# Q products of three chunks of layer 2 in a seven-product form, and other queue orders in which VectorE's and GpSimd's norms exclude each other

## The chip, the cores and the metric

The kernel runs on one core of one Trainium2 chip. The metric is device time in microseconds, the median of several executions. The core has five engines with their own instruction queues: TensorE (matmuls, PE in the profile; PEld are its weight loads), VectorE (DVE), ScalarE (ACT), GpSimd (POOL) and SyncE (SP), which issues the DMAs here. They meet only at semaphores.

## The reference

Four layers on 2048 tokens of 512 features: linear attention with 32 heads of 16, a feed-forward block with 1376 hidden features, and the same two again with the same weights. Each has a layernorm ahead of it and adds its result to x.

```python
qkv = (x @ wqkv).reshape(B, S, 3, H, Dh).transpose(2, 0, 3, 1, 4)
q, k, v = qkv[0], qkv[1], qkv[2]
phi = lambda t: where(t > 0, t + 1, exp(t)) + 1e-6
pq, pk = phi(q), phi(k)
kv = einsum("bhsd,bhse->bhde", pk, v)
z = einsum("bhsd->bhd", pk)
num = einsum("bhqd,bhde->bhqe", pq, kv)
den = einsum("bhqd,bhd->bhq", pq, z)[..., None] + 1e-6
attention = (num / den).transpose(0, 2, 1, 3).reshape(B, S, D) @ wo

x = x + attention(layernorm(x), wqkv, wo)
x = x + maximum(layernorm(x) @ w1, 0) @ w2
x = x + attention(layernorm(x), wqkv, wo)
return x + maximum(layernorm(x) @ w1, 0) @ w2
```

## The kernel before

Everything stays in SBUF. The 2048 tokens are 16 tiles of 128, in 4 chunks of 512. Layers are numbered 0 to 3: 0 and 2 are attention, 1 and 3 feed-forward. In names such as `2.q1_3` the first number is the layer; then come chunk and block. Tiles: `xn` holds normalized tokens (tokens on partitions), `Tb` the same transposed, `big` the results of the chunk at hand (phi(K), phi(Q), hidden units, and four spare units of a chunk, `rb_unit`), `ps` the eight PSUM banks, `escr` scratch, `Mf` the 512x512 matrix that the attention's end multiplies with.

**An attention layer.** Per chunk: K (`a_k`, four groups of four 512-column matmuls, `Tb` stationary), Q (`a_q`, four groups, `wqkv` stationary, all 512 tokens of the chunk as columns), and the sums G = xn^T phi(K) (`a_g`). phi takes three or four operations (`phi_evac`): ScalarE writes t + 1 (`_lin`) and exp(t) (`_exp`) from PSUM, VectorE cuts the exponential (`_em`) and takes the larger (`_phi`). When all K are done, G goes through wv (`a_kv`, into a bank from which VectorE's masked copy makes `KVT`, `kvmask`) and through wo (`a_m`) into `Mf`. The divisors are products with `Zc` (`a_den`), ScalarE's ln and exp of them (`lnd`, `rdc`), a DMA that spreads them over partitions (`spread`), and a multiplication of phi(Q) (`pqs`). Then `a_fin_chunk` multiplies with `Mf` and adds to x.

**A feed-forward layer.** The second product (`b_out_chunk`), and the first one of six of the eight chunks (`b_h_halves`), are done in a seven-product form: a product of 2 x 2 blocks with seven block products instead of eight, with sums of the operands' blocks made ahead on VectorE (`fs_`, `ts`, `ws_`, `sw`). One unit of it takes two banks Y and R and a chain: products 1 and 5 into Y, two copies by ScalarE (one of them seeds R), products 2 and 6, an addition on VectorE in PSUM, products 3 and 7, another addition, product 4. Two banks of results come out.

**The order.** The program records every operation with what it reads and writes, and `_list_schedule` makes the queue of each engine: on each, strictly by `prio`, which is an operation's place in the program plus its entry in the table `HINTS` (about 1700 entries). The table `ON` says on which of two engines a movable operation runs (evacuations with relu, norms, copies of G). Of VectorE's operations it marks some as `lock` and of GpSimd's some as `hog`: in the planner's clock a `lock` that would start during a `hog` begins at its end. Nothing at run time enforces that; there are only the queues and the semaphores.

The operations of two neighbouring layers are interleaved: layer 2's first chunks are on TensorE while layer 1's last are.

Of the kernel before, what the change touches and what calls it, by code (L numbers as in the profile page):

```python
# [7 lines left out]
ALU = alu_op_type.AluOpType  # L8
# [53 lines left out]
C_DVE_SC = 520.0  # L62
H_PLAIN = {(3, 0): 2}
# [7 lines left out]
HINTS = {"0.ainv": 7469, "0.ainvs": 7592, "0.apos": 6448, "0.apow": 6789, "0.apows": 7312, "0.as1": -3606, "0.as3": 3550, "0.as_h1":  # L71
# [377 lines left out]
def _list_schedule(ops, tile_ops, vbank, nbanks=8, full=(), seeded=()):  # L449
# [45 lines left out]
    while remaining:  # L495
# [78 lines left out]
        else:  # L574
            q = pool_op[0]
            held = 0.0
            if o.lock and q is not None and q.hog and q.t_start < st < q.t_done - TAIL[POOL]:
                held = q.t_done - TAIL[POOL] - st
# [1313 lines left out]
```

## Time and profile before

| | us |
|---|---|
| median of 3 runs (lowest, highest) | 267.24 (267.15, 267.86) |
| the profiled execution, its own time | 267.75 |
| its span, first to last instruction | 266.0 |
| TensorE busy, matmuls (1890) | 260.9 |
| VectorE busy (557 instructions) | 215.4 |
| ScalarE busy (420) | 192.0 |
| GpSimd busy (131) | 51.2 |

The granted TensorE clock was 1.000 over the span. The page cuts the span into 40 slices, a digit for the busy tenths of each (9 is 90% or more):

```profile
PE   7999999999999999999999999999999999999996
DVE  4897986799889999879786848479999888697865
ACT  4798899998975756898718689578599974656300
POOL 6410010012860023400001340001734040000000
```

A row of the groups reads: line, engine, operation, out<-in, shapes, count, busy us and mean ns of one, idle time of the engine ahead of them and what ended it. A row of the timeline reads: start, length, engine, line, operation, shapes, count, and in brackets the idle time ahead of it. A row of a window reads: the stretch, its length, and for PE, PEld, DVE, ACT and POOL the busy us with the count; then the clock and the DMA's share. Matmul rows include the pipeline's tail, so that neighbouring rows overlap.

### The profile page before, as it was taken

Reading aid. Unit: us, or ns where it says so; the run is one execution under the profiler, and the core shown is the slowest. Engines: PE = TensorE matmul, PEld = TensorE weight load, DVE = VectorE, ACT = ScalarE, POOL = GpSimd, SP = SyncE. Lnnn points to the kernel's source line nnn. Section 1 sums busy time; section 2 is a strip of 40 time slices with the busy share of each in tenths; the row PEclk is TensorE's granted clock in tenths of the full one; section 3 lists DMA queues with packets and bytes.
Section 4 is the critical chain, followed back from the end, with each engine's and each line's share of the span. In section 5 each row is a group of like instructions: output and inputs, shape, how many; then the busy total and the mean of one; then the engine's idle time right before and its main releaser. Section 6 shows DMA issues by size and latency. Waiting matters only on the chain.

```text
span 266.0 us, 5120 instructions
## 1 busy us (share of the span) xinstructions
PE 260.9 (98%) x1890; PEld 171.2 (64%) x1890; DVE 215.4 (81%) x557; ACT 192.0 (72%) x420; POOL 51.2 (19%) x131
## 2 busy tenths in 40 slices
PE   7999999999999999999999999999999999999996
PEld 3344444644755888767776744474488888888874
DVE  4897986799889999879786848479999888697865
ACT  4798899998975756898718689578599974656300
POOL 6410010012860023400001340001734040000000
PEclk9999999999999999999999999999999999999999
DMA  6744489866249023150000313054460501602104
GB/s 213 252 88 81 139 159 366 229 156 100 44 87 160 0 21 58 25 99 1 2 0 0 66 27 68 4 140 111 107 120 2 99 2 38 140 2 70 52 1 160
DMA packets 48122, 23.22 MB, mean 87 GB/s; under 512 B 38784, under 2 KB 45920, under 8 KB 48096
## 3 DMA queue, kind: packets, MB, share of 16 engines
q1 hardware_dynamic: 48096, 22.88, 37.2%
q8 instruction: 15, 0.25, 0.4%
q14 instruction: 11, 0.09, 0.1%
HBM read 7.14 MB, written 2.10 MB: 35 GB/s over the span
## 4 chain that ended last, share of the span: by engine, by line
PE 91%; DMA 4%; DVE 3%; SPq 1%; issue 0%; DVEq 0%
PE ps L928 91%; DMA xin<-in_A_x_dram 3%; DMA Tb<-xn 1%; DVE bst L802 1%; DVE big L921 1%; DVE xn L845 0%; DVE wqkv L944 0%; SPq L750 0%; SPq L744 0%; DVE escr L914 0%; DVE xn L1610 0%; DVE mv L803 0%; DVE veps L809 0%; DVEq L1822 0%
## 5 line engine op out<-in xcount | busy, mean ns | idle before, releaser
L928 PE MATMUL ps<-Tb,w 128*128 128x256 f16 (+2 forms) x240 | 42.0, 301 | 0.0
L1327 ACT ACTIVATE big<-ps 128x512 bf16<-128x512 f32 x58 | 33.0, 597 | 10.3 <-PE ps L928 10.0
L960 ACT ACTIVATE sqscr<-xres 128x512 bf16<-128x512 f32 x48 | 29.9, 626 | 9.6 <-DVE xres L954 9.4
L928 PE MATMUL ps<-w,big 128*128 128x256 bf16 (+5 forms) x213 | 36.5, 293 | 0.0
L928 PE MATMUL ps<-wqkv,Tb 128*128 128x512 bf16 x144 | 34.5, 379 | 0.9 <-DMA wqkv<-in_A_wqkv_dram 0.6
L928 PE MATMUL ps<-big,xn 128*128 128x512 bf16 (+1 forms) x160 | 31.2, 336 | 0.2 <-DVE veps L809 0.2
L910 ACT ACTIVATE big<-ps 128x512 bf16<-128x512 f32 x48 | 28.7, 603 | 1.5 <-PE ps L928 1.4
L928 PEld LDWEIGHTS ps<-Tb,w 128*128 128x128 f16 (+1 forms) x240 | 23.2, 98 | 9.3
L928 PE MATMUL ps<-xn,xin 128*128 128x256 f16 x168 | 28.8, 272 | 0.0
L1274 DVE TENSOR_TENSOR ps<-ps,escr 128x256 f32<-128x256 f32 x56 | 22.8, 427 | 7.1 <-PE ps L928 6.6
L912 ACT ACTIVATE escr<-ps 128x512 bf16<-128x512 f32 x44 | 25.7, 604 | 3.4 <-PE ps L928 3.3
L928 PE MATMUL ps<-Tb,wqkv 128*128 128x512 bf16 x112 | 27.1, 379 | 0.0
L825 POOL TENSOR_SCALAR mean<-s 128x4 f32<-128x4 f32 (+1 forms) x13 | 3.7, 285 | 117.4 <-DVE xres L954 117.3
L928 PE MATMUL ps<-Mf,big 128*128 128x512 bf16 x112 | 25.0, 379 | 0.0
L928 PEld LDWEIGHTS ps<-wqkv,Tb 128*128 128x128 bf16 x144 | 13.7, 98 | 16.5 <-DMA wqkv<-in_A_wqkv_dram 1.1
L928 PEld LDWEIGHTS ps<-w,big 128*128 128x128 bf16 (+1 forms) x213 | 20.3, 98 | 5.2
L928 PEld LDWEIGHTS ps<-big,xn 128*128 128x128 bf16 x160 | 15.1, 98 | 12.1 <-POOL xn L979 0.7
L928 PE MATMUL ps<-xin,big 128*128 128x256 bf16 x150 | 20.8, 272 | 0.0
L914 DVE TENSOR_SCALAR escr<-escr 128x512 bf16<-128x512 bf16 x52 | 14.3, 286 | 6.7 <-ACT escr L912 6.5
L928 PEld LDWEIGHTS ps<-Mf,big 128*128 128x128 bf16 x112 | 10.7, 98 | 12.7 <-DVE big L1105 0.3
L921 DVE TENSOR_TENSOR big<-big,escr 128x512 bf16<-128x512 bf16 x46 | 18.4, 417 | 0.2
L928 PEld LDWEIGHTS ps<-Tb,wqkv 128*128 128x128 bf16 x112 | 10.8, 98 | 11.7 <-issue 0.4
(139 smaller groups left out, 499.4 us busy)
## 6 DMA issues: line engine op xcount, KB each, us to landing
big<-rdc SPq DMA_DIRECT2D x32, 128.0 KB, 2.7
wqkv<-in_A_wqkv_dram SPq DMA_DIRECT2D x3, 512.0 KB, 5.0
w<-in_B_w_dram SPq DMA_DIRECT2D x1, 1376.0 KB, 7.6
w<-in_B_w_dram SPq DMA_DIRECT2D x1, 1280.0 KB, 10.8
xin<-in_A_x_dram SPq DMA_DIRECT2D x2, 512.0 KB, 4.5
out_dram<-wqkv SPq DMA_DIRECT2D x2, 512.0 KB, 3.5
xin<-in_A_x_dram SPq DMA_DIRECT2D x2, 256.0 KB, 6.2
wo<-in_A_wo_dram SPq DMA_DIRECT2D x1, 512.0 KB, 7.6
```

The costliest lines, as they stand in the source:

```text
L802: g.add(DVE, lambda e: e.bn_stats(bst[:, i, :], xin[:, i, :]), [("xin", i)] + list(after), [("bst", i)], C_DVE_BNST, name="bnst%d" % i)
L825: g.add(POOL, lambda e: e.tensor_scalar(mean[:, sl], s1[:, sl], -INV_D, None, ALU.mult), [("s1", i) for i in tl], [("mean", i) for i in tl ...
L910: g.add(ACT, lambda e: e.activation(dst_ap, psv[:, b, :], ACTF.Identity, bias=1.0 + 1e-6, scale=sc), [("ps", b)] + rk, [dst_key], C_ACT_PS ...
L912: g.add(ACT, lambda e: e.activation(esc, psv[:, b, :], ACTF.Exp, scale=sc), [("ps", b)] + rk, [ekey], C_ACT_EXP + xd, name=name + "_exp")
L914: g.add(DVE, lambda e: e.tensor_scalar(esc, esc, 1.0, 1e-6, ALU.min, ALU.add), [ekey], [ekey], C_DVE_BF4X, name=name + "_em")
L921: g.add(DVE, lambda e: e.tensor_tensor(dst_ap, dst_ap, esc, ALU.max), [dst_key, ekey], [dst_key], 340.0, name=name + "_phi")
L928: last = e.matmul(o, l, r, start=st, stop=sp, skip_group_check=skip)
L960: g.add(ACT, lambda e: e.activation(sqscr[:, q, :], xres[:, i, :], ACTF.Square, accum_out=s2[:, i:i + 1]), [("xres", i)], [("sqscr", q), ( ...
L1274: g.add(DVE, lambda e: e.tensor_tensor(psv[:, bank, 256:512], psv[:, Y, 0:256], m5, ALU.add), [("ps", Y), ("escr", s)], [("ps", bank)], C_ ...
L1327: g.add_flex([(ACT, lambda e: e.activation(unit_ap(u), psv[:, b, :], ACTF.Relu), C_ACT_PSUM), (DVE, lambda e: e.tensor_scalar(unit_ap(u), ...
```

## The change

1. In layer 2 the Q products of chunks 0, 1 and 2 (`QS`) take the seven-product form: `qk_chunk` in place of `a_q`. The blocks are: features in halves (0 to 255, 256 to 511), output columns in halves, and tokens of the chunk in halves. A chunk is two units (`qk_unit`, c = 0 and 1), each of which makes two of the four blocks of 128 output columns for all 512 tokens. The sums of the weights (`qk_weight_sums`, `swq1` to `swq4`, bf16, into `Mf`) are made once, during layer 1; the sums of the tokens (`qk_token_sums`, `ts0_1` and so on) for each of the three chunks, into the spare units of `big`. Chunk 3's Q, all K (`KS` is empty) and layer 0 stay as they were.
2. The planner marks every VectorE norm as `lock` (before, only those under 345 ns by its table, the norms of layer 0's start), only where the operation really runs on VectorE, and GpSimd's memset and selects of the start as `hog`. It takes 2100 instead of 1700 ns for the load of half of wq and wk, and 1000 instead of 800 for one load of x.
3. `HINTS` and `ON` are new throughout, so the order on every engine differs in all four layers.

```diff
--- before.py
+++ after.py
+KS = ()
+QS = (0, 1, 2)
...
-HINTS = {"0.ainv": 7469, "0.ainvs": 7592, "0.apos": 6448, "0.apow": 6789, "0.apows": 7312, "0.as1": -3606, "0.as3": 3550, "0.as_h1":
...
+HINTS = {"0.ainv": 7056, "0.ainvs": 9513, "0.apos": 6691, "0.apow": 7029, "0.apows": 7087, "0.as1": -9951, "0.as3": 4807, "0.as_h1":
...
-        self.lock = eng == DVE and dur < 345.0 and (name.endswith(("_em", "_phi")) or name[:4] in ("cent", "norm", "wvle")) or eng == DVE and (name[:3] in ("fs_", "ws_", "ts0", "ts1", "ts2", "ts3") or name[:2] == "sw" or name[:3] == "wsc")
-        self.hog = eng == POOL and name[:4] in ("norm", "fs_0", "fs_1", "fs_2", "fs_3")
+        self.lock = eng == DVE and dur < 345.0 and (name.endswith(("_em", "_phi")) or name[:4] in ("cent", "wvle")) or eng == DVE and (name[:4] == "norm" or name[:3] in ("fs_", "ws_", "ts0", "ts1", "ts2", "ts3") or name[:2] == "sw" or name[:3] == "wsc")
+        self.hog = eng == POOL and name[:4] in ("norm", "fs_0", "fs_1", "fs_2", "fs_3", "ms_h", "as_h")
...
-            if o.lock and q is not None and q.hog and q.t_start < st < q.t_done - TAIL[POOL]:
+            if e == DVE and o.lock and q is not None and q.hog and q.t_start < st < q.t_done - TAIL[POOL]:
...
-                [], [("wk", k), ("wq", k)], 1700.0, "ld_wqk%d" % k, late=(0.0, 300.0)[k])
-        ld_x(1, 0, 2, 800.0)
+                [], [("wk", k), ("wq", k)], 2100.0, "ld_wqk%d" % k, late=(0.0, 300.0)[k])
+        ld_x(1, 0, 2, 1000.0)
...
+        def qk_w(kind, k):
+            off, sums, key = (0, Mf, "Mf") if kind == "q" else (D, rdc, "rdc")
+            if k in (1, 2, 4):
+                d0, f0 = {1: (0, 0), 2: (2, 0), 4: (2, 256)}[k]
+                return wqkv[:, d0:d0 + 2, off + f0:off + f0 + 256], [("w" + kind, d0 // 2)]
+            q = {3: 4, 5: 1, 6: 2, 7: 3}[k]
+            return sums[:, q - 1, :].rearrange("p (d n) -> p d n", n=256), [(key, q - 1)]
...
+        def qk_weight_sums(kind):
+            off, key = (0, "Mf") if kind == "q" else (D, "rdc")
+            lf, ll, hf, hl = (wqkv[:, d:d + 2, off + f:off + f + 256] for d in (0, 2) for f in (0, 256))
+            lo, hi = [("w" + kind, 0)], [("w" + kind, 1)]
+            sm = {q: qk_w(kind, {4: 3, 1: 5, 2: 6, 3: 7}[q])[0] for q in range(1, 5)}
+            for q, a, b, op, rd in ((1, ll, hl, ALU.add, lo + hi), (3, lf, ll, ALU.subtract, lo),
+                                    (2, sm[1], lf, ALU.subtract, lo + [(key, 0)]), (4, hf, sm[2], ALU.subtract, hi + [(key, 1)])):
+                g.add(DVE, lambda e, q=q, a=a, b=b, op=op: e.tensor_tensor(sm[q], a, b, op), rd, [(key, q - 1)], C_DVE_TSUM, name="sw%s%d" % (kind, q))
+
+        def qk_block(t, r, c):
+            return Tb[:, 4 * t + 2 * c:4 * t + 2 * c + 2, 2 * r:2 * r + 2, :]
...
+        def qk_ts(t, q):
+            return unit_ap(rb_unit(t, q - 1)).rearrange("p (i d k) -> p i d k", i=2, d=2)
+
+        def qk_token_sums(t):
+            def flat(ap):
+                return ap.rearrange("p i d k -> p i (d k)")
+            lo, hi = qk_keys(t, 0), qk_keys(t, 1)
+            for q, a, b, rd in ((1, qk_block(t, 0, 1), qk_block(t, 0, 0), lo + hi), (2, qk_block(t, 1, 1), qk_ts(t, 1), hi + [("big", rb_unit(t, 0))]),
+                                (4, qk_block(t, 1, 0), qk_ts(t, 2), lo + [("big", rb_unit(t, 1))]), (3, qk_block(t, 1, 1), qk_block(t, 0, 1), hi)):
+                g.add(DVE, lambda e, q=q, a=a, b=b: e.tensor_tensor(flat(qk_ts(t, q)), flat(a), flat(b), ALU.subtract), rd, [("big", rb_unit(t, q - 1))],
+                      C_DVE_TSUM, name="ts%d_%d" % (t, q))
+
+        def qk_unit(t, kind, c):
+            Y, R = alloc_bank(True), alloc_bank(seeded=True)
+            s = scr_state["e"] % NSCR
+            scr_state["e"] = (s + 1) % NSCR
+            m5 = escr[:, s, :].bitcast(F32)
+            tag = "%s%d_%d" % (kind, t, c)
+
+            def prod(k, bank, half, start=False):
+                if k in (1, 2, 3):
+                    r_, c_ = {1: (0, 0), 2: (1, 0), 3: (1, 1)}[k]
+                    x, xk = qk_block(t, r_, c_), qk_keys(t, c_)
+                else:
+                    q = {4: 4, 5: 1, 6: 2, 7: 3}[k]
+                    x, xk = qk_ts(t, q), [("big", rb_unit(t, q - 1))]
+                w, wk = qk_w(kind, k)
+
+                def mk():
+                    o = psv[:, bank, 256 * half:256 * half + 256]
+                    if kind == "q":
+                        return [(o, w[:, d, 128 * c:128 * c + 128], x[:, :, d, :], start and d == 0, False, True) for d in range(2)]
...
+                mm_group(mk, xk + wk, [("ps", bank)], 2 * C_MM256, "%sp%d_%d_%d" % (kind, t, c, k))
...
+            def add(bank, n):
+                g.add(DVE, lambda e: e.tensor_tensor(psv[:, bank, 256:512], psv[:, Y, 0:256], m5, ALU.add),
+                      [("ps", Y), ("escr", s)], [("ps", bank)], C_DVE_HALF, name="%sa%d" % (tag, n))
+
+            def evac(bank, h):
+                if kind == "q":
+                    u = pq_unit(c + 2 * h, t)
+                    phi_evac(bank, unit_ap(u), ("big", u), "q%d_%d" % (t, c + 2 * h))
+                    return
...
+            def s0():
+                prod(1, Y, 0, True)
+                prod(5, Y, 1)
+                copy(lambda: psv[:, R, 0:256], 0, [("ps", Y)], [("ps", R)], tag + "c")
+                copy(lambda: m5, 1, [("ps", Y)], [("escr", s)], tag + "m")
+
+            def s1():
+                prod(2, R, 0)
+                prod(6, Y, 0)
+                add(R, 0)
+
+            def s2():
+                prod(3, R, 1)
+                prod(7, Y, 0)
+                evac(R, 0)
+                add(Y, 1)
+
+            def s3():
+                prod(4, Y, 0)
+                evac(Y, 1)
+            return s0, s1, s2, s3
+
+        def qk_chunk(t, kind):
+            a, b = qk_unit(t, kind, 0), qk_unit(t, kind, 1)
+            for f in (a[0], a[1], b[0], a[2], b[1], a[3], b[2], b[3]):
+                f()
...
                 def p1(t):
-                    for i in FIRST_ORDER if t == 0 and first_layer else range(4 * t, 4 * t + 4):
-                        a_k(i)
+                    if not first_layer and (t in KS or t in QS):
+                        qk_token_sums(t)
+                    if not first_layer and t in KS:
+                        qk_chunk(t, "k")
+                    else:
+                        for i in FIRST_ORDER if t == 0 and first_layer else range(4 * t, 4 * t + 4):
+                            a_k(i)
...
+                        return
+                    if not first_layer and t in QS:
+                        qk_chunk(t, "q")
                         return
                     a_q(t)
...
                 def o_step(t):
                     if layer == 1 and t == 0:
                         scale_weights()
+                    if layer == 1 and t == 0:
+                        for kind, used in (("k", KS), ("q", QS)):
+                            if used:
+                                qk_weight_sums(kind)
                     b_out_chunk(t, last_layer)
```

More of the change, by code (lines that the diff above doesn't have):

```diff
@@ L580, in _list_schedule @@
             o.t_done = st + o.dur + held + TAIL[e]
-            if o.lock:
+            if e == DVE and o.lock:
                 if st + held > train[1] + 10.0:
@@ L587, in _list_schedule @@
             q = pool_op[0]
-            if q is not None and (o.lock and not held or e == POOL):
+            if q is not None and (e == DVE and o.lock and not held or e == POOL):
                 fin = q.t_done - TAIL[POOL]
@@ L895, in transpose_pe, with phi_evac @@
             part(0, 4, ("T", i), str(i))
-        def phi_evac(b, dst_ap, dst_key, name, tok=None):
+        def phi_evac(b, dst_ap, dst_key, name, tok=None, shaped=lambda a: a):
+            dst_keys = dst_key if isinstance(dst_key, list) else [dst_key]
             n_scr = NSCR + NSCR0 if g.layer == 0 else NSCR
@@ L909, in phi_evac @@
             if not stt:
[L910 to L911 removed]
+                g.add(ACT, lambda e: e.activation(dst_ap, shaped(psv[:, b, :]), ACTF.Identity, bias=1.0 + 1e-6, scale=sc),
+                      [("ps", b)] + rk, dst_keys, C_ACT_PSUM + xd, name=name + "_lin")
             g.add(ACT, lambda e: e.activation(esc, psv[:, b, :], ACTF.Exp, scale=sc),
```

22 lines of the change are left out of this document (15 added, 7 removed), and 554 rows, old and new, of tables (HINTS, ON).

## The prediction

> **What bounds the kernel now.** I read the page's head first, then the chain of waits, then who waits for whom on TensorE, then the order of time where a term needs a price.
>
> ```profile
> span 266.0 us, 5120 instructions
> PE 260.9 (98%) x1890; PEld 171.2 (64%) x1890; DVE 215.4 (81%) x557; ACT 192.0 (72%) x420; POOL 51.2 (19%) x131
> ...
> 16.75 3.86 DMA Tb<-xn
> ...
> 20.65 242.27 PE ps L928 x1790
> ...
> PE ps L928 <- DMA Tb<-xn: 0.3, 1, 0.3
> ...
> PEld ps L928 <- DVE ps L1274: 0.5, 3, 0.2
> ```
>
> A busy share of 98% alone proves little, since the ends of matmuls are modelled. The chain says more: after the transpose that lands at 20.65 it consists of 1790 TensorE instructions in one piece, 242.27 us long. In the list of waits from 20.65 on, TensorE itself has one entry, 0.3 us, that same transpose. The weight loads do wait (0.5 us for the additions of the existing seven-product units, three times), but a weight load runs ahead of its matmul, and the matmul stream shows no gap. So the time is: start-up, plus the matmul columns, plus a tail. Fewer columns shorten it one for one; a wait of the matmul stream lengthens it one for one; VectorE and ScalarE cost nothing until TensorE waits for them.
>
> **The change, part by part: the columns.** The Q products of chunks 0 to 2 in layer 2 are 12 groups of four 512-column matmuls, 48 in all. In their place stand 6 units of 7 products of 2 matmuls of 256 columns, 84 in all.
>
> ```profile
> 22.39 3.62 PE L928 MATMUL ps<-Tb,wqkv 128*128 128x512 bf16 x16
> 25.84 1.03 PE L928 MATMUL ps<-big,xn 128*128 128x512 bf16 x4
> ...
> 174.35 1.47 PE L928 MATMUL ps<-big,xn 128*128 128x256 bf16 x12
> 175.66 0.28 PE L928 MATMUL ps<-GT,wqkv 128*128 128x128 bf16 x2
> ```
>
> Each row's length includes the pipeline's tail, so I go from start to start. Sixteen Q matmuls of layer 0 take 25.84 − 22.39 = 3.45 us, 0.2156 each; twelve of 256 columns take 1.31 us, 0.1092 each. Removed 48 × 0.2156 = 10.35, added 84 × 0.1092 = 9.17: **−1.18 us**. Half of 0.2156 per 256 columns would make it −1.29; that is its other end.
>
> The Trainium skill, "TensorE: Matmul & The Clock Gate", section "Back-to-back issue gap", speaks against this: it gives a sustained spacing of 131 ns at 512 columns and 81 ns at 128, and calls the 216 ns of a 512-column matmul an isolated figure. By a straight line between its two figures (98 ns at 256, an estimate) the exchange would be 84 × 98 − 48 × 131 ns = +1.9 us. The trace disagrees: 0.2156 in a stream of sixteen.
>
> **The den products.** The divisor's products (on Zc) run four at a time on quarters of the array, and have a fixed cost for each block of them.
>
> ```profile
> 170.78 1.02 PE L928 MATMUL ps<-big,xn 128*128 128x512 bf16 x4
> 171.74 0.83 PE L928 MATMUL ps<-big,Zc 128*32 128x512 bf16 x12
> 172.50 1.04 PE L928 MATMUL ps<-Tb,wqkv 128*128 128x512 bf16 x4
> ...
> 181.64 1.03 PE L928 MATMUL ps<-Mf,big 128*128 128x512 bf16 x4
> 182.60 0.40 PE L928 MATMUL ps<-big,Zc 128*32 128x512 bf16 x4
> 182.93 3.41 PE L928 MATMUL ps<-Mf,big 128*128 128x512 bf16 x15
> ```
>
> Four matmuls at 0.2156 should hand over at 171.64; the block starts at 171.74 and hands over at 172.50. So twelve cost 0.86, of which 3 × 0.2156 is streaming and 0.21 is the change of form. The single group: 182.50 to 182.93, 0.43 = 0.2156 + 0.21. TensorE at the end of layer 2, before:
>
> ```order
> L928 MATMUL ps<-ident,GT 128x1 x4
> L928 MATMUL ps<-big,xn 128x512 x4
> L928 MATMUL ps<-big,Zc 32x512 x12
> L928 MATMUL ps<-Tb,wqkv 128x512 x4
> L928 MATMUL ps<-big,xn 128x512 x4
> ```
>
> and now, from the same products to the first one on wo:
>
> ```order
> L943 MATMUL ps<-big,Zc 32x512 x8
> L943 MATMUL ps<-big,xn 128x256 x4
> L943 MATMUL ps<-big,wqkv 128x256 x2
> L943 MATMUL ps<-big,xn 128x256 x4
> L943 MATMUL ps<-GT,wqkv 128x128 x2
> L943 MATMUL ps<-big,xn 128x512 x4
> L943 MATMUL ps<-Tb,wqkv 128x512 x4
> L943 MATMUL ps<-big,Zc 32x512 x4
> L943 MATMUL ps<-big,xn 128x256 x4
> L943 MATMUL ps<-GT,wqkv 128x128 x10
> L943 MATMUL ps<-big,xn 128x256 x4
> L943 MATMUL ps<-wo,KVT 128x512 x2
> ```
>
> One block of twelve became eight and four; with the last group that is three blocks in place of two: **+0.21**.
>
> **A tight place behind it.** The first product on wo needs the mask that VectorE writes (into KVT). VectorE ahead of the first mask, before:
>
> ```order
> L1017 CAST GT<-ps 128x256
> L921 TENSOR_TENSOR big<-big,escr 128x512
> L1105 TENSOR_TENSOR big<-big 128x512
> L1030 TENSOR_TENSOR KVT<-ps,bmask 128x256
> L914 TENSOR_SCALAR escr<-escr 128x512
> ```
>
> and now:
>
> ```order
> L1026 CAST GT<-ps 128x512
> L1032 CAST GT<-ps 128x256
> L929 TENSOR_SCALAR escr<-escr 128x512 x2
> L1045 TENSOR_TENSOR KVT<-ps,bmask 128x256
> L936 TENSOR_TENSOR big<-big,escr 128x512
> ```
>
> Two tensor_scalar on exponentials moved ahead of the mask; the second waits for ScalarE's exponential of the Q block q3_0. Counting from the first den: TensorE has, by the rows just shown and the prices above (0.055 for 128 columns, from x2 in 0.11), 8 dens 0.64, 4 + 2 + 4 of 256 1.09, 2 of 128 0.11, 8 of 512 1.72, 4 dens 0.43, 4 + 4 of 256 0.87, 10 of 128 0.55: 5.4 us until wo. ScalarE has seven operations on that path (ln, exp, exp, ln, exp, exp, exp).
>
> ```profile
> 172.19 0.60 ACT L1087 ACTIVATE lnd<-ps 128x512 f32<-128x512 f32 x1 [1.09 <-PE ps L928]
> ...
> 176.13 0.58 ACT L910 ACTIVATE big<-ps 128x512 bf16<-128x512 f32 x1
> ...
> 177.93 0.42 DVE L1030 TENSOR_TENSOR KVT<-ps,bmask 128x256 bf16<-128x256 f32 x1
> 178.34 0.29 DVE L914 TENSOR_SCALAR escr<-escr 128x512 bf16<-128x512 bf16 x1
> ```
>
> Before, the like seven took 176.13 − 172.19 = 3.94 us, starting 0.45 after the first den (171.74). Then 0.29 and 0.42 on VectorE, and some 0.25 to TensorE (mask end 178.35, first wo product 178.60): 5.35. It fits by 0.05; one more ScalarE operation ahead (0.6) makes it late. I take **+0.1**, from 0 to +0.6.
>
> **Start-up.** VectorE before:
>
> ```order
> L1610 TENSOR_SCALAR xn<-xin,mv,rstd 128x512 x2
> L888 COPY Tb<-ps 128x512
> L802 BN_STATS bst<-xin 128x6 x2
> L803 BN_AGGR mv<-bst 128x2 x2
> L914 TENSOR_SCALAR escr<-escr 128x512
> ```
>
> and now:
>
> ```order
> L1728 TENSOR_SCALAR xn<-xin,mv,rstd 128x512
> L902 COPY Tb<-ps 128x512
> L1728 TENSOR_SCALAR xn<-xin,mv,rstd 128x512
> L816 BN_STATS bst<-xin 128x6 x2
> L817 BN_AGGR mv<-bst 128x2 x2
> L929 TENSOR_SCALAR escr<-escr 128x512
> ```
>
> The norm of tile 1 moved from the middle of the busy stretch to ahead of the statistics of chunk 1, and tile 0's norm ahead of the centering of tile 2.
>
> ```profile
> 8.96 5.79 PE L928 MATMUL ps<-wqkv,Tb 128*128 128x512 bf16 x26 [0.60 <-DMA wqkv<-in_A_wqkv_dram]
> 14.95 3.19 PE L928 MATMUL ps<-big,xn 128*128 128x512 bf16 x16 [0.20 <-DVE veps L809]
> ...
> 9.58 1.29 DVE L802 BATCH_NORM_STATS2 bst<-xin 128x6 f32<-128x512 bf16 x2 [1.18 <-DMA xin<-in_A_x_dram]
> 13.94 0.40 DVE L1610 TENSOR_SCALAR xn<-xin,mv,rstd 128x512 bf16<-128x512 bf16 x1
> 14.26 0.24 DVE L803 BATCH_NORM_AGGREGATE mv<-bst 128x2 f32<-128x6 f32 x2
> ```
>
> VectorE idles 1.18 us ahead of 9.58, and from there works without a break to the last norm of chunk 1, which releases the transpose at 16.75. The moved norm takes 14.26 − 13.94 = 0.32 of that stretch and now fills the hole, so the transpose can be issued up to 0.32 earlier. ScalarE holds part of it back: the exponential of k2 is now seventh in its queue, no longer fourth. That later centering (by one norm, some 0.33) falls on TensorE ahead of 8.96, where it waits 0.60 for the weights. I take **−0.15**, from −0.32 to +0.1.
>
> **VectorE and ScalarE.** Added on VectorE: 12 token sums and 4 weight sums (nearest row: the existing sums, 0.415) and 12 additions in PSUM (0.427): 16 × 0.415 + 12 × 0.427 = 11.8 us. On ScalarE: 12 copies of half a bank, 4.6 us.
>
> ```profile
> L1237 DVE TENSOR_TENSOR xn<-Tb 128x512 f16<-128x512 f16 x12 | 4.9, 415 | 0.5 <-DMA Tb<-xn 0.5
> L1274 DVE TENSOR_TENSOR ps<-ps,escr 128x256 f32<-128x256 f32 x56 | 22.8, 427 | 7.1 <-PE ps L928 6.6
> L1271 ACT ACTIVATE escr<-ps 128x256 f32<-128x256 f32 x28 | 10.4, 388 | 3.6 <-PE ps L928 3.6
> L1327 ACT ACTIVATE big<-ps 128x512 bf16<-128x512 f32 x58 | 33.0, 597 | 10.3 <-PE ps L928 10.0
> L1328 DVE TENSOR_SCALAR big<-ps 128x512 bf16<-128x512 f32 x22 | 14.5, 683 | 2.2 <-PE ps L928 2.2
> ...
> 200.00:210.00 10.00, 10.00 (x100) 8.65 (x98) 9.72 (x23) 9.78 (x27) 2.86 (x6) 1.00 0.23 44
> 100.00:150.00 50.00, 50.00 (x393) 37.30 (x392) 41.13 (x103) 36.74 (x84) 8.72 (x22) 1.00 0.13 25
> 150.00:180.00 30.00, 30.00 (x183) 15.76 (x182) 19.11 (x54) 23.52 (x48) 3.23 (x10) 1.00 0.33 70
> ```
>
> By the new order chunk 0's units and chunk 1's sums fall into 100 to 150: 13 operations, 5.4 us. The table ON also moves a net six evacuations of layer 1's chunks 2 and 3 to ScalarE (0.683 off VectorE, 0.597 onto ScalarE each, by the last two groups): VectorE 41.1 + 5.4 − 4.1 = 42.4 of 50, ScalarE 36.7 + 1.5 + 3.6 = 41.8. In 150 to 180 VectorE gets 12 more (5.1): 24.2 of 30, ScalarE 23.5 + 3.1 and one evacuation of G: 27.2. In 200 to 210 both engines were over 97% busy and TensorE still did not wait. So I cost all of it at 0; without that cover it is the slower rival's price.
>
> **Norms that exclude each other.**
>
> ```profile
> 156.59 1.45 DVE L850 TENSOR_SCALAR xn<-xres,mean,rstd 128x512 bf16<-128x512 f32 x2 [2.95 <-POOL nbias L839]
> 156.53 0.77 POOL L850 TENSOR_SCALAR xn<-xres,mean,rstd 128x512 bf16<-128x512 f32 x1
> 149.13 0.54 DVE L850 TENSOR_SCALAR xn<-xres,mean,rstd 128x512 bf16<-128x512 f32 x1
> ```
>
> Two norms take 1.45 beside GpSimd's, where one alone takes 0.54: about 0.4 us of VectorE are lost. But no matmul waits at any layer's boundary now, so keeping them apart saves VectorE time and gains 0 on the path.
>
> **Sum.** −1.18 + 0.21 + 0.10 − 0.15 = −1.02 us. The profiled execution's span goes from 266.0 to 265.0. That execution took 267.75 with what lies around the span, the median of the runs is 267.24; I take the difference off the median: 266.2.
>
> **Rivals.** *The saving is eaten* (within 0.3%, about what a measurement of this kernel can tell from no change, 0.8 us). Six units have three handovers each to other engines. If six of the 18 are late by 0.2, the longest wait of that kind in the list, that is 1.2 and the time is 267.4. For it: the 0.05 of slack above. Against it: 28 such units run now without a gap.
>
> *VectorE's queue holds TensorE* (slower). The additions of chunk 0 stand between the feature sums of layer 1's chunk 2, which wait for that chunk's last relu, 0.82 each:
>
> ```profile
> L1389 DVE TENSOR_TENSOR xn<-big 128x1280 bf16<-128x1280 bf16 x7 | 5.7, 818 | 1.3 <-ACT big L1327 1.3
> ```
>
> If two of the four additions come a whole sum late (1.6) and chunks 1 and 2 lose 0.3 each behind ordinary evacuations, the net is 2.2 − 1.0 = +1.2: 268.4; all four late, 269.5. It decides once the waits pass 1.8 us. Against it: the loads above leave 15% free.
>
> *Weight loads bind.*
>
> ```profile
> L928 PEld LDWEIGHTS ps<-Tb,w 128*128 128x128 f16 x144 | 13.9, 98 | 2.1
> ```
>
> Weights are loaded 84 times instead of 48, at 98 ns each. If the 36 more were exposed: 3.5 − 1.0 = +2.5, 269.7. Against it: the twelve 256-column matmuls above, each with its own load, keep 0.109. Chance 0.02. A spacing set by both operations is also what the Trainium skill states in the section named above; the sixteen and the twelve matmuls here do not show it.
>
> *The change only reorders*: if the planner's order put as much idle time elsewhere, it would show as the first rival.
>
> **Chances.** Forecast 0.64, saving eaten 0.17, VectorE 0.17, weight loads 0.02. The forecast's own range is 265.6 (start-up −0.32, no tight place, −1.29, and 0.3 of spread) to 266.6; a twentieth of it lies above 266.44. Faster 0.61, same 0.20 (with the forecast's rest), slower 0.19. The range reaches to the slower case's price: 265.6 to 268.4.
>
> **What would show it.** Right: the chain still one piece of TensorE, ending about 1.0 earlier; 48 rows of 512 columns fewer at 0.2156; two den blocks of eight and four; the transpose of the start landing before 20.6. Wrong: TensorE entries in the list of waits after start-up that name the additions, the token sums or the mask; a gap between the second and third pair of products of a unit; a stretch between 100 and 180 with a PE busy below its length.

## The result and the profile after

The changed kernel takes 266.25 us in the median (266.12 to 267.14, 14 runs), the kernel before 267.39 beside it (267.15 to 267.86, 14 runs). The ratio is 0.9961, with a 95% interval from 0.9953 to 0.9969: 0.8 to 1.3 us less, 1.04 in the middle. The profiled execution of the changed kernel took 267.05 us with a span of 265.3; x landed late in it, as the part on the start shows.

The head of the page after:

```profile
span 265.3 us, 5230 instructions
PE 260.8 (98%) x1926; PEld 174.0 (66%) x1926; DVE 222.8 (84%) x578; ACT 201.3 (76%) x439; POOL 49.7 (19%) x131
```

and its chain of waits (start, length, what):

```profile
8.89 178.51 PE ps L943 x1221
187.40 0.02 issue
187.42 74.82 PE ps L943 x661
```

The chain is TensorE from 8.89 on and ends at 187.42 + 74.82 = 262.24, where it ended at 20.65 + 242.27 = 262.92 before: 0.68 earlier. VectorE has 7.4 us more work than before, ScalarE 9.3, and the end follows neither.

TensorE's matmuls by form, the rows that the change touches (count, busy us, mean ns of one):

```profile
L943 PE MATMUL ps<-Tb,wqkv 128*128 128x512 bf16 x64 | 15.3, 379 | 0.0
L943 PE MATMUL ps<-big,Mf 128*128 128x256 bf16 x36 | 6.7, 273 | 0.0
L943 PE MATMUL ps<-Tb,wqkv 128*128 128x256 bf16 x24 | 4.4, 273 | 0.0
L943 PE MATMUL ps<-Tb,Mf 128*128 128x256 bf16 x12 | 2.3, 273 | 0.0
L943 PE MATMUL ps<-big,wqkv 128*128 128x256 bf16 x12 | 2.3, 272 | 0.0
```

48 of the 112 matmuls with 512 columns on `wqkv` are gone, and 36 + 24 + 12 + 12 = 84 with 256 columns have come.

TensorE and its weight loads in order of time, at the places that the prediction speaks of and at those where it now waits:

```profile
153.38 1.03 PE L943 MATMUL ps<-wqkv,Tb 128*128 128x512 bf16 x4
...
154.40 0.11 PEld L943 LDWEIGHTS ps<-big,Mf 128*128 128x128 bf16 x2 [0.49 <-DVE ps L1128]
154.41 0.39 PE L943 MATMUL ps<-big,Mf 128*128 128x256 bf16 x2
...
171.20 0.38 PE L943 MATMUL ps<-big,Mf 128*128 128x256 bf16 x2
171.51 0.62 PE L943 MATMUL ps<-big,Zc 128*32 128x512 bf16 x8
172.06 0.61 PE L943 MATMUL ps<-big,xn 128*128 128x256 bf16 x4
...
176.43 0.60 PE L943 MATMUL ps<-big,xn 128*128 128x256 bf16 x4
176.89 0.60 PE L943 MATMUL ps<-wo,KVT 128*128 128x512 bf16 x2
...
179.72 2.50 PE L943 MATMUL ps<-Mf,big 128*128 128x512 bf16 x10
182.14 0.40 PE L943 MATMUL ps<-big,Zc 128*32 128x512 bf16 x4
```

The list of waits has no entry of TensorE after the start, and yet three waits stand here. Four matmuls from 153.38 should hand over at 153.38 + 4 × 0.2156 = 154.24; the next row starts at 154.41, and the weight load ahead of it waited for line 1128, an addition of a Q unit: 0.16 (the rows are rounded). Ten from 179.72, and 0.10 for the edge of a den block, end at 181.98, and that block starts at 182.14: 0.16 (it lies inside the ten, ahead of the matmul at 181.60). A matmul's row is 0.38 long while the next one can follow after 0.2156; the first 0.16 of a wait lie under the modelled end and are in no list of idle times. The third, 0.18 ahead of 187.42, is seen only by the 0.02 beyond that, the "issue" at which the chain breaks. Such waits are read from start to start.

### The profile page after: what moved, and what is told of

The parts are those of the page before. It is cut to its first block, busy times and chain, and to the rows that moved or that the text cites. A ratio compares the mean times of both kernels' runs of the same rounds, so it can differ in the third digit from the quotient of the medians.

```text
span 265.3 us, 5230 instructions
## 1 busy us (share of the span) xinstructions
PE 260.8 (98%) x1926; PEld 174.0 (66%) x1926; DVE 222.8 (84%) x578; ACT 201.3 (76%) x439; POOL 49.7 (19%) x131
## 4 chain that ended last, share of the span: by engine, by line
PE 95%; DVE 2%; DMA 1%; issue 0%; SPq 0%; DVEq 0%
PE ps L943 95%; DMA xin<-in_A_x_dram 1%; DVE bst L816 0%; DVE wqkv L959 0%; DVE xn L1728 0%; DVE xn L1672 0%; SPq L758 0%; DVE Tb L902 0%; DVE mv L817 0%; DVEq L1952 0%
## 5 line engine op out<-in xcount | busy, mean ns | idle before, releaser
L1445 ACT ACTIVATE big<-ps 128x512 bf16<-128x512 f32 x59 | 33.7, 598 | 11.9 <-PE ps L943 11.6
L943 PE MATMUL ps<-Tb,w 128*128 128x256 f16 (+2 forms) x240 | 42.4, 301 | 0.0
L943 PE MATMUL ps<-w,big 128*128 128x256 bf16 (+5 forms) x213 | 35.6, 293 | 0.0
L943 PE MATMUL ps<-big,xn 128*128 128x512 bf16 (+1 forms) x160 | 32.6, 337 | 0.0
L927 ACT ACTIVATE escr<-ps 128x512 bf16<-128x512 f32 x44 | 26.4, 614 | 5.7 <-PE ps L943 5.5
L925 ACT ACTIVATE big<-ps 128x512 bf16<-128x512 f32 x48 | 29.0, 616 | 1.6 <-PE ps L943 1.4
L943 PE MATMUL ps<-xn,xin 128*128 128x256 f16 x168 | 30.0, 273 | 0.0
L943 PE MATMUL ps<-Tb,wqkv 128*128 128x512 bf16 (+1 forms) x88 | 19.7, 350 | 0.0
L943 PEld LDWEIGHTS ps<-xn,xin 128*128 128x128 f16 x168 | 16.2, 98 | 2.8 <-ACT ps L1389 0.2
```

The source lines that it names most:

```text
L925: g.add(ACT, lambda e: e.activation(dst_ap, shaped(psv[:, b, :]), ACTF.Identity, bias=1.0 + 1e-6, scale=sc), [("ps", b)] + rk, dst_keys, C ...
L927: g.add(ACT, lambda e: e.activation(esc, psv[:, b, :], ACTF.Exp, scale=sc), [("ps", b)] + rk, [ekey], C_ACT_EXP + xd, name=name + "_exp")
L943: last = e.matmul(o, l, r, start=st, stop=sp, skip_group_check=skip)
L1445: g.add_flex([(ACT, lambda e: e.activation(unit_ap(u), psv[:, b, :], ACTF.Relu), C_ACT_PSUM), (DVE, lambda e: e.tensor_scalar(unit_ap(u), ...
```

## Experiments

In the experiments the order is written out as each operation's own place in the program, which gives the same queues; `MOVED` then gives single operations another place. The times, with the kernel before run beside them (267.5 to 267.6 in the sessions of the experiments, 267.39 in that of the changed kernel):

| kernel | median, us (runs) | ratio to the kernel before | 95% | stretch, us |
|---|---|---|---|---|
| changed kernel | 266.25 (14) | 0.9961 | 0.9953 to 0.9969 | 0 |
| plain Q products in the new orders | 268.84 (9) | 1.0043 | 1.0028 to 1.0058 | +1.80 |
| norm of tile 1 moved back | 266.43 (6) | 0.9954 | 0.9938 to 0.9970 | −0.01 |
| kernel before, that norm moved | 267.60 (12) | 1.0002 | 0.9989 to 1.0015 | +0.32 |
| seventh product left out | 264.99 (6) | 0.9903 | 0.9879 to 0.9928 | −1.11 |
| one more den block | 266.44 (12) | 0.9965 | 0.9947 to 0.9982 | +0.22 |
| one more norm on VectorE | 266.85 (12) | 0.9971 | 0.9956 to 0.9986 | +0.47 |
| additions doubled | 268.86 (10) | 1.0058 | 1.0036 to 1.0081 | +2.62 |
| idle work behind the additions | 272.72 (5) | 1.0195 | 1.0175 to 1.0215 | +6.33 |
| additions left out | 266.11 (6) | 0.9940 | 0.9920 to 0.9960 | −0.16 |
| five operations moved | 266.17 (6) | 0.9946 | 0.9930 to 0.9962 | −0.21 |
| six moved | 265.93 (7) | 0.9943 | 0.9921 to 0.9964 | −0.31 |
| five and two norms moved | 266.81 (12) | 0.9974 | 0.9959 to 0.9989 | +0.45 |

The intervals are 0.7 to 1.3 us wide (0.4 for the changed kernel), and medians of two sessions differ by 0.1 to 0.2 for the same kernel, so a term of a few tenths is read from the traces and not from these times. The last column does that. It is TensorE's stretch in the profiled execution, from the start of its first product behind the transposes of the start (20.30 in the changed kernel) to the start of its last product (262.63), less the changed kernel's 242.33; it leaves out the start, in which loads land at other times in each execution. For the kernel before it is +0.33.

**Where the gain is: the columns.** Two kernels. The first has the changed kernel's orders and plain Q products:

```diff
-QS = (0, 1, 2)
+QS = ()
...
+MOVED = {"2.qproj0_0": <place of 2.qp0_0_3>, "2.qproj0_1": <place of 2.qp0_1_3>, "2.qproj0_2": <place of 2.qp0_0_4>, ...}
```

> The orders of the changed kernel are kept, the Q products of the three chunks are plain again: eight 512-column matmuls a chunk and group of 256 columns where 14 of 256 columns stood, so 48 matmuls of 512 columns come back and 84 of 256 go; the token sums, the weight sums, the Q additions and the Q copies on VectorE and ScalarE are gone. Theory (the gain is the columns taken off TensorE, 48 x 0.2156 - 84 x 0.1092 = 1.18 us): about 267.4 us, 1.0 to 1.3 above the changed kernel. Rival (the queue orders alone make the gain): about 266.3, no difference.

It takes 268.84, 2.6 above the changed kernel and 1.2 above the one before. The rival falls: without the seven-product form these orders are a loss. But the theory's number is too small by 1.4. In its trace TensorE waits, from start to start, at three places where the changed kernel does not: 0.24 near 112, 0.20 near 143 and 0.30 near 150.2, and the wait of 0.16 at 154 is gone. 1.18 + 0.74 − 0.16 = 1.76 accounts for the stretch, 1.80. The profiled execution was the fastest of the nine, at 268.19; why the median lies 0.65 above it no trace shows. The orders are made for the other shape of the Q work, so this kernel does not measure the columns by themselves. The second does:

```diff
                 prod(3, R, 1)
-                prod(7, Y, 0)
                 evac(R, 0)
```

> The changed kernel without the seventh product of the six Q units, 12 matmuls of 256 columns less (that part of the Q projection of three chunks of layer 2 is left out). Theory (columns taken off TensorE come off the time one for one): 266.25 - 12 x 0.1092 = 264.9 us. Rival (what TensorE saves in these units is spent waiting for the additions or the loads): 265.7 to 266.3.

264.99, 1.26 below the changed kernel, where 12 × 0.1092 is 1.31 (by the ratios it is 1.5, so the closeness is partly chance). The trace adds up: −1.31 for the columns, −0.16 for the wait at 154, which is gone, and +0.37 for new waits (0.07 at 157.60, 0.30 in two pieces at 231.5) make −1.10, and the stretch is 1.11 shorter. Columns that go off TensorE come off its stretch one for one.

**The den blocks.** One TensorE group is moved, so that a block of eight becomes two of four:

```diff
+MOVED = {"2.den1": <behind 2.g2a_2>}
```

> The changed kernel with one TensorE operation moved: the second denominator group of layer 2 goes behind the next matmul group instead of directly behind the first, so that four blocks of one-row matmuls stand in layer 2 where three stood. Theory (each block costs TensorE about 0.21 at its two edges, whatever is in it): 266.45 us, 0.2 above the changed kernel. Rival (only the matmuls in it count): 266.25.

266.44, which agrees and would not settle it alone; the stretch is 0.22 longer. TensorE in its trace, in order of time:

```profile
170.66 0.40 PE L908 MATMUL ps<-big,Zc 128*32 128x512 bf16 x4
170.99 0.61 PE L908 MATMUL ps<-big,xn 128*128 128x256 bf16 x4
171.53 0.40 PE L908 MATMUL ps<-big,Zc 128*32 128x512 bf16 x4
171.86 0.39 PE L908 MATMUL ps<-big,wqkv 128*128 128x256 bf16 x2
```

Four of 256 columns between the blocks take 4 × 0.1092 = 0.44, from 170.99 to 171.43; the block starts 0.10 later. It hands over after 171.86 − 171.53 = 0.33, of which 0.2156 is streaming: 0.11. Each block costs 0.21 at its two edges, for four matmuls as for eight.

**The start.** One norm back, and the same norm moved in the kernel before:

```diff
 # changed kernel
+MOVED = {"0.norm1": <behind 0.bnst7>}
 # kernel before
+MOVED = {"0.norm1": <ahead of 0.bnst4>, "0.rstd_1": <ahead of 0.as_h2>}
```

> The changed kernel with one operation moved: the first norm of tile 1 of layer 0 goes back behind the last statistics of that tile group in VectorE's queue, where it stood before the change. Theory (the start is shorter because this norm fills a hole in VectorE's queue): 266.4 to 266.6 us, 0.15 to 0.36 above the changed kernel. Rival (the start is set by the loads of x): 266.25, no difference.

> The kernel before with one part of the change alone: the first norm of tile 1 of layer 0 stands ahead of the fourth statistics in VectorE's queue, as the change has it. Theory (it takes two short waits of TensorE at the start away): 267.1 us, 0.15 to 0.36 below the kernel before. Rival (the start is set by the loads): 267.4, no difference.

Neither moved the time by more than the noise. In the kernel before the rival's number came, 267.60 beside 267.63, though the interval leaves room for 0.3 of the theory's 0.15 to 0.36. In the changed kernel 266.43 lies in the theory's range by the median and on the rival's side by the ratio, 0.9954, so it decides nothing. The executions differ in when x lands, so the start is measured from the statistics of tile 2 (which wait for it) to the product of K of tile 7, the first one behind the DMA transpose. VectorE and TensorE in the changed kernel:

```profile
5.22 0.69 DVE L816 BATCH_NORM_STATS2 bst<-xin 128x6 f32<-128x512 bf16 x1 [0.94 <-DMA xin<-in_A_x_dram]
14.97 3.20 PE L943 MATMUL ps<-big,xn 128*128 128x512 bf16 x16
20.30 1.90 PE L943 MATMUL ps<-wqkv,Tb 128*128 128x512 bf16 x8
```

in the changed kernel with the norm back:

```profile
4.28 0.69 DVE L781 BATCH_NORM_STATS2 bst<-xin 128x6 f32<-128x512 bf16 x1
14.45 3.20 PE L908 MATMUL ps<-big,xn 128*128 128x512 bf16 x16
19.65 1.89 PE L908 MATMUL ps<-wqkv,Tb 128*128 128x512 bf16 x8
```

and in the kernel before with the norm moved:

```profile
4.27 0.69 DVE L769 BATCH_NORM_STATS2 bst<-xin 128x6 f32<-128x512 bf16 x1
14.36 3.20 PE L895 MATMUL ps<-big,xn 128*128 128x512 bf16 x16
20.14 1.90 PE L895 MATMUL ps<-wqkv,Tb 128*128 128x512 bf16 x8 [0.42 <-DMA Tb<-xn]
```

That is 15.08, 15.37 and 15.87; the kernel before needs 20.65 − 4.66 = 15.99. So the new orders are 0.6 to 0.9 shorter here, with that norm in either place, and the norm alone brings the old ones 0.1. In the other ten profiles of the new orders the stretch is 15.0 to 15.5, but for one of 16.15, in which the weights of layer 0 landed later. So later loads are in this stretch too, and only its second part, from the sums G (the row of sixteen) on, is free of them: 5.33, 5.20 and 5.78 in these three, 5.70 in the kernel before, and 5.2 to 5.3 in all twelve profiles of the new orders. There the new orders are 0.4 to 0.6 shorter. TensorE waits for the transpose 0.51 and 0.58 from start to start in the old ones, 0 to 0.14 in the new. These rows show too why the profiled execution of the changed kernel took 267.05: x landed about 0.9 later in it than in these. What the first part owes to the orders was not isolated. With the second part goes the time that the two transposes of this stretch (DMA, Tb from xn) take from issue to landing. The kernel before:

```profile
DMA to landing us min/median/max: 3.1/3.5/3.9
```

the changed kernel:

```profile
DMA to landing us min/median/max: 3.1/3.3/3.4
```

The longer one takes 3.8 to 3.9 in both profiles of the old orders and 3.2 to 3.4 in all twelve of the new ones. Fifteen of its sixteen completions come 3.1 to 3.2 behind its issue in all fourteen; the last comes 0.73 and 0.76 behind them in the old orders, 0.06 to 0.26 in the new. Something else on the DMA engines goes with that. Each profile has a load of instructions there (one packet of 8192 bytes, 0.3 to 0.5 us). In the old orders it starts among the transpose's packets, at 19.23 and 18.71, and the last four or five of these end just behind it, at 19.58 and 19.07, where the others were done by 19.34 and 18.83. In the new ones it starts within 0.02 of the last packet's end, or later. No run moved the one against the other, so that this is the cause is not shown.

**Norms that exclude each other.** The norm of tile 12 of layer 1, which the change has on ScalarE, on VectorE again:

```diff
-"1.norm12": 1,
+"1.norm12": 0,
...
+MOVED = {"1.norm12": <ahead of 1.norm13>}
```

> The changed kernel with the norm of tile 12 of layer 1 on VectorE again, ahead of that of tile 13, instead of on ScalarE, so that two norms of VectorE fall together with GpSimd's norm of tile 15. Theory (a norm that runs beside a GpSimd norm takes 0.9 us instead of 0.54, and what is queued behind it holds TensorE by that much): the wait of TensorE near 154 us grows from 0.16 to about 0.5, 266.6 us. Rival (these norms are never on the path): 266.25.

The changed kernel in order of time, GpSimd and VectorE around 153:

```profile
152.51 0.77 POOL L864 TENSOR_SCALAR xn<-xres,mean,rstd 128x512 bf16<-128x512 f32 x1
152.63 1.38 DVE L864 TENSOR_SCALAR xn<-xres,mean,rstd 128x512 bf16<-128x512 f32 x2
153.93 0.42 DVE L1128 TENSOR_TENSOR ps<-ps,escr 128x256 f32<-128x256 f32 x1
```

and with the third norm on VectorE:

```profile
152.63 0.78 POOL L829 TENSOR_SCALAR xn<-xres,mean,rstd 128x512 bf16<-128x512 f32 x1
152.74 1.85 DVE L829 TENSOR_SCALAR xn<-xres,mean,rstd 128x512 bf16<-128x512 f32 x3
154.51 0.42 DVE L1093 TENSOR_TENSOR ps<-ps,escr 128x256 f32<-128x256 f32 x1
154.99 0.39 PE L908 MATMUL ps<-big,Mf 128*128 128x256 bf16 x2 [0.47 <-DVE ps L1093]
```

The addition stands behind the norms in VectorE's queue, and TensorE's next product waits for it: 0.63 from start to start (0.47 and the 0.16 under the tail) in place of 0.16, 0.47 more, where the theory had some 0.34 (266.85, 0.6 above). The third norm lies behind GpSimd's, so this shows that the norms in the queue hold the addition, and not what the clash does. Of the two norms the first lasts 0.93 beside GpSimd's, where one alone lasts 0.54, so the clash is 0.39 of this queue, more than the wait of 0.16. That the wait would go without the clash is worked out from this, not run.

**How much VectorE's cover holds.** Three kernels. The additions doubled:

```diff
             def add(bank, n):
+                g.add(DVE, lambda e: e.tensor_tensor(psv[:, bank, 256:512], psv[:, Y, 0:256], m5, ALU.add),
+                      [("ps", Y), ("escr", s)], [("ps", bank)], C_DVE_HALF, name="%sa%dx" % (tag, n))
                 g.add(DVE, lambda e: e.tensor_tensor(psv[:, bank, 256:512], psv[:, Y, 0:256], m5, ALU.add),
```

> The changed kernel with each of the 12 Q additions on VectorE written twice (the second one adds the same operand again, so the Q products of layer 2 and what follows from them are not the reference's): 12 x 0.43 = 5.1 us more on VectorE, beside the other queues. Theory (VectorE's additions are covered by TensorE's stream): 266.3 us, at most 0.3 above the changed kernel. Rival (VectorE is near its limit between 100 and 180 us and holds TensorE): 267.3 or more.

268.86, 2.6 above, for 5.2 us more in VectorE's rows: the theory falls. TensorE waits from start to start at seven places, 0.28 to 0.46 each, six of them at products of the Q units that need an addition. That could be the short way from an addition to its product, or VectorE's queue as a whole. So idle work was put behind each addition, for which no product waits:

```diff
+                for z in "yz":
+                    g.add(DVE, lambda e: e.tensor_tensor(m5, m5, m5, ALU.max),
+                          [("escr", s)], [("escr", s)], C_DVE_HALF, name="%sa%d%s" % (tag, n, z))
```

> The changed kernel with two idle VectorE operations (the larger of an operand and itself, which changes nothing) right behind each of the 12 Q additions: they load VectorE's queue by 5 us or more, as the doubled additions did, but no product waits for them directly. The doubled additions cost 2.6 us. Theory (that cost was the short way from an addition to the next product into the same bank, and not VectorE's load): at most 1.0 above the changed kernel, 266.3 to 267.2. Rival (VectorE's load holds TensorE there, whichever operation it is): 268.8, as with the doubled additions.

272.72, 6.5 above. The 24 idle operations (L1096) are 10.6 us of VectorE's rows, 440 ns each. The longest of TensorE's waits between 100 and 185 (us in total, times, longest):

```profile
PE ps L908 <- DVE ps L1093: 1.5, 3, 0.9
PE ps L908 <- DVE xres L924: 1.1, 1, 1.1
PE ps L908 <- DVE big L1062: 0.9, 1, 0.9
```

The load was twice that of the doubled additions, 10.6 us against 5.2, and TensorE now waits for whatever VectorE does next: an addition (L1093), an addition to x (L924), a token sum (L1062). So this theory falls too, and the trace speaks for the queue: 2.6 / 5.2 = 0.5 and 6.5 / 10.6 = 0.6 us for each microsecond added. One more entry of that list, 0.7, names a copy of ScalarE (L1090); whether ScalarE's own load holds TensorE no run tried. Then the other way, without the 12 additions:

```diff
                 prod(6, Y, 0)
-                add(R, 0)
...
                 evac(R, 0)
-                add(Y, 1)
```

> The changed kernel without its 12 Q additions on VectorE (their part of the Q products of layer 2 is left out): 5.1 us less on VectorE. Theory (in the changed kernel's own order the additions just fit beside TensorE's work, and only what is put on top of them costs time): TensorE loses its wait of 0.16 near 154 us and nothing else, 266.1 us. Rival (VectorE's load holds TensorE already, at half a microsecond for each microsecond of VectorE as the added operations showed): 263.7.

266.11, 0.14 below by the medians and 0.56 by the ratios. The trace decides for the theory: the wait of 0.16 near 154 is the only one that is gone, and the stretch is 0.16 shorter. So the additions cost 0.16 in these orders, by the norms ahead of one of them; but on top of them there is no room. The windows show where (stretch, length, busy us with counts of PE, PEld, DVE, ACT and POOL), in the changed kernel:

```profile
112.00:118.00 6.00, 6.00 (x49) 4.59 (x48) 5.77 (x13) 5.90 (x15) 0.00 (x0) 1.00 0.41 79
118.00:124.00 6.00, 6.00 (x50) 4.61 (x48) 5.74 (x17) 5.86 (x13) 0.00 (x0) 1.00 0.06 13
```

and with the additions doubled:

```profile
118.00:124.00 6.00, 5.52 (x42) 3.57 (x39) 5.90 (x18) 5.17 (x11) 0.00 (x0) 1.00 0.00 1
```

VectorE is busy 96% of these 12 us while four additions of chunk 0, its token sums and layer 1's feature sums pass through it, and ScalarE is busy 98%. With VectorE filled to 98%, TensorE is idle for 0.48 of the second six beyond its tails, and waits 0.90 in it from start to start (0.45 in two pieces at 120.3 and 120.6, 0.45 at 122.51).

**The three short waits.** Five operations moved by a place or two:

```diff
+MOVED = {"1.norm13": <behind 2.q1_1a0>, "2.pqs2_0": <ahead of 2.resid4>, "2.q3_2_lin": <behind 2.mev3>,
+         "2.q3_2_phi": <behind 2.pqs1_2>, "2.den3": <behind 2.fin2_2>}
```

> The changed kernel with five operations of VectorE and ScalarE moved by one or two places, each ahead of or behind a neighbour, so that three short waits of TensorE in layer 1 and layer 2 (0.16, 0.17 and 0.18 us in the profiled execution) have their operand earlier. Theory (they are on the chain that ends last, and of every execution): 265.75 us, 0.3 to 0.5 below the changed kernel. Rival (they belong to one execution, or the next operand is late instead): 266.25, no difference.

266.17. All three waits are gone from its trace, and one of 0.33 from start to start (0.17 beyond the tail) stands at 190.08, at the first product of chunk 3 of Q, which needs the last of four scaled pieces. TensorE there:

```profile
190.08 2.12 PE L908 MATMUL ps<-Mf,big 128*128 128x512 bf16 x9 [0.17 <-DVE big L1188]
```

So the rival holds in its second half: 0.50 was taken away and 0.33 came back. A sixth move:

```diff
+MOVED = {..., "2.resid7": <behind 2.pqs3_0>}
```

> The kernel with five moved operations, and a sixth moved: the addition to the residual of tile 7 in layer 2 goes behind the last scaled Q piece of the fourth chunk, so that the three pieces are ready 0.6 us sooner. In the kernel with five moves TensorE waited 0.33 us there, where it had waited 0.18 us earlier before. Theory (that wait goes and no other takes its place): 265.9 us, 0.3 below the kernel with five moves, 0.5 below the changed kernel. Rival (the chain through the weights' denominators sets this place): 266.2, no difference.

265.93, the fastest of the kernels that leave nothing out: 0.9943 of the kernel before (0.9921 to 0.9964), which overlaps the changed kernel's interval. The wait at 190 is gone; 0.22 in three pieces came at the start of layer 3, where the norms behind the moved operation are late. The other repair was worse:

```diff
+MOVED = {<the five>, "2.norm1": <behind 2.pqs3_0>, "2.norm0": <behind 2.norm1>}
```

> The kernel with five moved operations, and two others moved: in layer 2 the norms of tiles 1 and 0 on VectorE go behind the last scaled Q piece of the fourth chunk, so that the pieces and the residual additions of tiles 5 and 7 all come sooner. Theory (TensorE's wait of 0.33 at the end of layer 2 goes, and layer 3's start isn't late, as it was when one residual addition was put back): 265.75 us, 0.5 below the changed kernel. Rival (these norms are late for layer 3): 266.2 or more.

266.81. The list of TensorE's waits in its trace names the new one:

```profile
PE ps L908 <- DMA Tb<-xn: 0.8, 1, 0.8
```

Layer 3's first products need the transposes of these two norms; put back by some 2 us, they were late by 0.98 (0.82 and the 0.16 under the tail).

## Why the prediction was right, point by point

**The bound** was named rightly: TensorE's chain, and columns that count one for one. The kernel without the seventh product shows it: with 1.31 for its columns, its stretch adds up to 0.01. The argument for it, that the stream shows no gap because TensorE is not in the list of waits, is weaker than it was put: waits under 0.16 are not in that list.

**Columns, −1.18.** The counts are 48 and 84, and the 256-column groups keep 0.11 from start to start, as in 171.20 and the rows around it. The other end, −1.29, and the exposed weight loads have nothing for them.

**Den blocks, +0.21.** Three blocks in layer 2 in place of two, each 0.21 at its edges; a block split once more cost 0.22 of the stretch. The Trainium skill, "TensorEngine Tiling (Array Packing)", section "Key Properties", says that a change of the tiling mode drains TensorE; the edges agree with it, 0.10 into a block and 0.11 out of it.

**The tight place at wo, +0.10.** Nothing to speak of came: the product on `wo` starts at 176.89, 4 × 0.1092 and some 0.02 behind the row at 176.43. The way to it was costed as 5.4 us on TensorE, from the first den, and it took 176.89 − 171.51 = 5.38. The step that failed is who ends last ahead of the mask. VectorE in the changed kernel:

```profile
175.60 0.52 DVE L929 TENSOR_SCALAR escr<-escr 128x512 bf16<-128x512 bf16 x2
176.41 0.43 DVE L1045 TENSOR_TENSOR KVT<-ps,bmask 128x256 bf16<-128x256 f32 x1 [0.29 <-PE ps L943]
```

The operations on the exponentials that were thought late were done at 176.12, and VectorE stood idle for 0.29 until TensorE's own product for the mask came. The mask ended at 176.84, 0.05 ahead of the product on `wo`; from mask to product 0.25 had been priced.

**Start-up, −0.15.** The sign was right and both the size and the reason were wrong. The norm in VectorE's hole brings 0.1 to 0.3 from x's landing on, within the spread of the profiles, and no measurable time in two experiments. The stretch up to the product behind the transpose is 0.6 to 0.9 shorter, and 0.4 to 0.6 of that lie behind the sums G for another reason: the second transpose lands 0.4 to 0.7 sooner after its issue, while the issue itself comes no sooner behind the sums (16.75 − 14.95 = 1.80 before, 16.86 − 14.97 = 1.89 after).

**VectorE and ScalarE at 0.** Right for the change as it stands: without the additions 0.16 of the stretch is saved. The busy sums were close, in this order VectorE 42.4 and 24.2, ScalarE 41.8 and 27.2 forecast; the windows after:

```profile
100.00:150.00 50.00, 50.00 (x414) 39.14 (x413) 43.18 (x115) 42.12 (x98) 9.30 (x25) 1.00 0.18 35
150.00:180.00 30.00, 30.00 (x201) 17.18 (x200) 22.28 (x61) 26.18 (x55) 2.99 (x9) 1.00 0.25 54
```

What failed is the sentence that these loads leave 15% free. They do over 50 us, and in the 12 us where the units of chunk 0 stand they leave 4%. The slower rival, VectorE's queue, was one change of a few microseconds away: the doubled additions are that rival, at 268.86 where its price was 268.4.

**The norms, 0 on the path.** Wrong in its reason. That no matmul waits at a layer's boundary was true of the order before; in the new one an addition stands behind the norms of layer 1, and is late by 0.16 at 154. With one more norm on VectorE it is 0.63, so keeping that one off VectorE is worth 0.47. Nor does the change keep the norms apart at run time: in the profiles GpSimd's still hold VectorE's for 0.64 us in two places, where it was 1.01 in five.

**The saving eaten** (six of 18 handovers late by 0.2) came true in part: one handover of a unit is late by 0.16, and two at the end of layer 2 by 0.16 and 0.18.

**The sum.** In place of −1.18 + 0.21 + 0.10 − 0.15 = −1.02 the traces give −1.18 + 0.21 + 0.50 for the three waits, and 0.14 in waits of hundredths that were not sorted out: −0.33 for the stretch behind the start. With −0.6 to −0.9 for the start that is −0.9 to −1.2, against −1.04 by the ratio and 267.39 − 266.25 = 1.14 by the medians. So some two thirds of the gain lie in the start, which had 0.15 in the sum, and of the 0.97 that columns and den blocks save, 0.64 went into waits, which had 0.10. That the sum came out is luck: two terms that were too small stand against each other. In the profiled pair the start is 15.99 − 15.08 = 0.91 shorter, but x landed 5.22 − 4.66 = 0.56 later, so the product behind the transpose starts 0.35 earlier; −0.35 − 0.33 = −0.68, and the chain ended 0.68 earlier. (The range's lower end, by its own terms, is 265.5 and not 265.6; nothing hangs on it.)

## What to carry to other kernels

Read a stream that seems full from start to start, since waits shorter than a matmul's modelled tail are in no list. Ask for the cover of added work in windows as short as the stretch in which it stands, and test it by adding as much again: here 5 us of additions cost 0.16, and the next 5 us cost 2.6. Where a start differs between two kernels, measure it from the landing of the load, which alone moved by up to 1.0 us from one execution to the next, and look for later loads in the same stretch.

## What the runs showed of the hardware that was not expected

GpSimd and VectorE in the kernel with five operations moved, where one norm of VectorE overlaps GpSimd's:

```profile
151.91 0.77 POOL L829 TENSOR_SCALAR xn<-xres,mean,rstd 128x512 bf16<-128x512 f32 x1
152.03 0.93 DVE L829 TENSOR_SCALAR xn<-xres,mean,rstd 128x512 bf16<-128x512 f32 x1
```

VectorE's norm takes 0.93 where it takes 0.54 alone. The Trainium skill, "SBUF — State Buffer", section "Who interferes with whom", says that VectorE and GpSimd share a pair of ports as an exclusive lock, and that against a VectorE instruction that takes this pair, as its `tensor_scalar` can, the second to start is blocked until the first has finished. That the second is slowed agrees. A block until GpSimd's end at 152.68 would put the end of VectorE's norm 0.54 later, at 153.22; it ended at 152.96, so it was held for 0.39 of the 0.65 that the two rows overlap. The other profiles say more. In all 32 places of the fourteen profiles where a norm of VectorE starts over 0.03 us behind one of GpSimd and the rows overlap by more than 0.26, it is held for the overlap less 0.26, to 0.01; in the 18 where they overlap by 0.23 or less it lasts its 0.54. In the two where both start within 0.01, VectorE's lasts 0.54 and GpSimd's row 1.03 in place of 0.77. That fits a second one that is held in full, up to a moment 0.26 ahead of the end of GpSimd's row, whose span is rough.

Of two DMA transposes with the same bytes, issued at the same place, the second took 3.8 to 3.9 us to land in the old orders and 3.2 to 3.4 in the new ones. The difference is in its last completion alone, and goes with a load of instructions that falls among its packets or behind them.
